# Seven half-size products for four fifths of one block's x^T phi(k), with operand sums on GpSimd and VectorE

## The chip, the cores and the metric

The kernel runs on one core of a Trainium2 chip. The metric is the device time of one execution in microseconds (us); lower is better. A core has five engines that matter here: TensorE (PE in the profile) multiplies matrices into the accumulation memory PSUM, VectorE (DVE), ScalarE (ACT) and GpSimd (POOL) work elementwise, and SyncE (SP) issues DMA transfers. Each engine works through its own queue in order, and semaphores let one wait for another. GpSimd does not read PSUM in this kernel; TensorE reads only SBUF, the memory in which all tiles lie.

## What is computed

Two linear-attention blocks, A and B, read the same input `A_x` and are mixed by a gate. Cut to what matters:

```python
# x: 2048 x 640, wqkv: 640 x 1920, wo: 640 x 640; 32 heads of width 20; all bf16
g = sigmoid((x * gate_w).sum(-1, keepdims=True))
def block(x, wqkv, wo):
    q, k, v = split_heads(x @ wqkv)
    phi = lambda t: where(t > 0, t + 1, exp(t)) + 1e-6
    pq, pk = phi(q), phi(k)
    kv  = einsum("bhsd,bhse->bhde", pk, v)        # per head, 20 x 20
    z   = einsum("bhsd->bhd", pk)
    num = einsum("bhqd,bhde->bhqe", pq, kv)
    den = einsum("bhqd,bhd->bhq", pq, z)[..., None] + 1e-6
    return merge_heads(num / den) @ wo
out = g * block(x, A_wqkv, A_wo) + (1 - g) * block(x, B_wqkv, B_wo)
```

## The kernel before, in words

The kernel never forms v. Since kv is the diagonal part of phi(k)^T x Wv, it computes the 640 x 640 matrix G^T = x^T phi(k) once a block (tile `GT`), multiplies it by Wv, keeps the diagonal heads (`KVT`), and folds `wo` into that (`M`). The output is then the normalised phi(q) times `M`.

The 2048 rows of x are 16 chunks of 128, the 640 columns five blocks of 128 (`DT`). `xn` holds x with its rows on the partitions, `xT` its transpose, `pk` phi(k) by chunks, `pqT[0]` and `pqT[1]` the transposed phi(q) of A and of B. Five stages follow one another for each block:

- `k_chunk` (16 times): ten matmuls (L182) give x Wk for a chunk. `phi` empties them: an exponential on ScalarE (L177), then on VectorE the TENSOR_SCALAR step L178 from SBUF to SBUF, and L179, which reads PSUM and that result. The temporary tile `e` has three buffers.
- `q_unit` (ten for each block): ten matmuls of 512 columns (L218), and the same `phi` on 1024 columns. For A, five units come in the middle of the k chunks, after chunk 7. The other five are in `q_pass`, with the gate's columns (`gate_pass`) and the column sums of phi(k) (`z_rows`, L259) after the first of them and `z_pass` after the third.
- `g_pass` (five for each block): one pass gives one 128-row block of x^T phi(k), 16 chunks by two halves of 320 columns, 32 matmuls (L240), and one ScalarE copy into `GT`.
- `rec_pass`: the denominators (L153), multiplied by a gate factor (L330) and inverted on VectorE (L335). `norm_unit`, five for each block, spreads the inverses by eight small matmuls over two PSUM slots (L377); two multiplies per unit (L393) normalise phi(q) in place. In one of the two ScalarE first copies the PSUM result to bf16 (L391), in the other VectorE reads PSUM itself. In `g_all` the units lie between passes and half passes of g.
- `p_diff` (VectorE), then block B's k chunks, between which `kvt_pass` and `m_unit` finish `KVT` and `M` of A.

PSUM is four slots of two banks. `ps` hands them out in turn, or by number: in `g_all` the passes use slots 0 and 1, `rec_pass` slot 2, the units slots 2 and 3. The last stage, the output product, is already done by Strassen's scheme (`Pair`, `p1` to `p7`), with operand sums on VectorE (`add_rows`, L340).

The order of the instructions is the planner's, by priority in the order of the program, except where `tc.manual_schedule()` fixes the order as written. SP issues the loads: three transfers fill the last 12 chunks of `xn` (L519), and the weights of later stages follow. GpSimd builds the identity, the masks and `E4` in the first 10 us (L129 and others) and has nothing after that.

Of the kernel before, what the change touches and what calls it, by code (L numbers as in the profile page):

```python
# [8 lines left out]
P = 128  # L9
FP32 = mybir.dt.float32  # L10
BF16 = mybir.dt.bfloat16
ACT = mybir.ActivationFunctionType
ALU = mybir.AluOpType

S, D, H = 2048, 640, 32
Dh = D // H
DT = D // P
ST = S // P
# [3 lines left out]
HF = D // 2  # L22
# [4 lines left out]
SH = S // 2  # L27
# [3 lines left out]
def kernel(  # L31
# [11 lines left out]
    nc = tc.nc  # L43
# [4 lines left out]
    persist = ctx.enter_context(tc.tile_pool(name="persist", bufs=1))  # L48
    wpool = ctx.enter_context(tc.tile_pool(name="wpool", bufs=1))
    work = ctx.enter_context(tc.tile_pool(name="work", bufs=2))  # L50
# [5 lines left out]
    def ps_raw(name, slot=None):  # L56

        if slot is None:
            slot = turn[0]
            turn[0] = (slot + 1) % 4  # L60
        return psum.tile([P, 4 * HB], BF16, tag=f"ps{slot}", name=name)

    def ps(name, slot=None):

        return ps_raw(name, slot).bitcast(FP32).rearrange("p (b n) -> p b n", b=2)

    xT = persist.tile([P, DT, S], BF16, name="xT")
    xn = persist.tile([P, ST, D], BF16, name="xn")
    pk = persist.tile([P, ST, D], BF16, name="pk")
    pqT = [persist.tile([P, DT, S], BF16, name=f"pqT{b}") for b in "AB"]  # L70
    GT = persist.tile([P, DT, D], BF16, name="GT")
    KVT = persist.tile([P, NJ, D], BF16, name="KVT")
    M = [persist.tile([P, DT, D], BF16, name=f"M{b}") for b in "AB"]
# [6 lines left out]
    gwr = persist.tile([P, DT, H], BF16, name="gwr")  # L80
    zero = persist.tile([P, HB], BF16, name="zero")
    grow = persist.tile([1, D], BF16, name="grow")
    D3 = persist.tile([P, DT, S // 2], BF16, name="D3")
    TM = [None] * 4
    ge = [persist.tile([P, 2 * RB], FP32, name=f"ge{b}") for b in "AB"]

# [10 lines left out]
    wq = [None, None]  # L97
# [7 lines left out]
    for n in range(1, NB):  # L105
# [3 lines left out]
        for c in range(DT):  # L109
            nc.sync.dma_start_transpose(  # L110
                out=xT[:, c, n * HB:(n + 1) * HB], in_=x2[n * HB:(n + 1) * HB, c * P:(c + 1) * P]
# [8 lines left out]
    for sign, base in ((1, 0), (-1, Dh - 1)):  # L120
        nc.gpsimd.affine_select(
            out=maskE[:], in_=maskE[:], pattern=[[sign * P, DT], [-sign * Dh, H]],
# [3 lines left out]
    for r in range(4):  # L126
        rows = slice(32 * r, 32 * r + 32)
        for sign, base in ((1, 0), (-1, Dh - 1)):
            nc.gpsimd.affine_select(  # L129
                out=E4[rows], in_=E4[rows], pattern=[[sign, D]],  # L130
# [43 lines left out]
    def phi(dst, src, n):  # L174

        e = work.tile([P, 2, n], BF16, tag="e", name="e", bufs=3)
        nc.scalar.activation(out=e[:], in_=src, func=ACT.Exp)  # L177
        nc.vector.tensor_scalar(e[:], e[:], 1.0, EPS, op0=ALU.min, op1=ALU.add)  # L178
        nc.vector.scalar_tensor_tensor(out=dst, in0=src, scalar=1.0 + EPS, in1=e[:], op0=ALU.add, op1=ALU.max)  # L179
# [32 lines left out]
    def q_unit(b, m, h):  # L212

        pt = ps(f"q{'AB'[b]}")
        for u in range(2):
            for c in range(DT):
                n = 2 * h + u
                nc.tensor.matmul(  # L218
                    pt[:, u, :], lhsT=wq[b][:, c, m * P:(m + 1) * P], rhs=xT[:, c, n * HB:(n + 1) * HB],
                    start=(c == 0), stop=(c == DT - 1),  # L220
                )
        phi(pqT[b][:, m, h * 2 * HB:(h + 1) * 2 * HB].rearrange("p (b n) -> p b n", b=2), pt, HB)

    def evac(dst, pt, eng):

        copy = nc.scalar.copy if eng == "act" else nc.vector.tensor_copy
        copy(out=dst.rearrange("p (b n) -> p b n", b=2), in_=pt[:, :, 0:HF])

    def g_pass(b, c, slot, between=None):

        pt = ps(f"g{'AB'[b]}", slot)
        for i in range(ST):
            if between is not None and i == ST // 2:
                between()
            for hf in range(2):
                g_mm(c, i, hf, pt)
        evac(GT[:, c, :], pt, "act")

    def g_mm(c, i, hf, pt):
        nc.tensor.matmul(  # L240
            pt[:, hf, 0:HF], lhsT=xn[:, i, c * P:(c + 1) * P], rhs=pk[:, i, hf * HF:(hf + 1) * HF],
            start=(i == 0), stop=(i == ST - 1),
        )
# [68 lines left out]
    def m_half(b, c, hf, dst):  # L312

        for k, j in enumerate((c, c + 1)):
# [3 lines left out]
                rhs=wo_sb[b][:rows, j, hf * HF:(hf + 1) * HF], start=(k == 0), stop=(k == 1),  # L318
            )

    def rec_pass(b, zsel, slot):

        pt = ps(f"den{'AB'[b]}", slot)
        for h in range(2):
            by_group(pt[:, 0, h * RB:(h + 1) * RB], zsel, pqT[b], h)
        rts = []
        for h in range(2):
            part = slice(h * RB, (h + 1) * RB)
            d1 = work.tile([P, RB], FP32, tag="d1", name="d1")
            nc.vector.scalar_tensor_tensor(  # L330
                out=d1[:], in0=pt[:, 0, part], scalar=EPS, in1=ge[b][:, part], op0=ALU.add, op1=ALU.mult
            )
            rT = work.tile([P, RB], BF16, tag="rT", name="rT")
            with nc.allow_low_precision(reason="a fp32 reciprocal, stored as the bf16 that multiplies bf16"):
                nc.vector.reciprocal(out=rT[:], in_=d1[:])  # L335
            rts.append(rT)
        return rts

    def add_rows(dst, a, b, op):
        nc.vector.tensor_tensor(out=dst, in0=a, in1=b, op=op)  # L340

    def p_diff():

        for rows in (slice(0, HB), slice(HB, SH)):
            up = slice(SH + rows.start, SH + rows.stop)
            add_rows(D3[:, :, rows], pqT[0][:, :, rows], pqT[0][:, :, up], ALU.subtract)

# [24 lines left out]
    def norm_unit(b, parts, rts, slots):  # L372

        pts = [ps(f"ex{'AB'[b]}", s) for s in slots]
        for k, (m, h) in enumerate(parts):
            for j in range(4):
                nc.tensor.matmul(  # L377
                    pts[j // 2][:, j % 2, k * RB:(k + 1) * RB], lhsT=E4[32 * j:32 * j + 32, m * P:(m + 1) * P],
                    rhs=rts[h][32 * j:32 * j + 32, :], start=True, stop=True,
                )  # L380
        (m0, h0), (m1, h1) = parts
        for jj in range(2):
            src = pts[jj][:].rearrange("p j (k n) -> p j k n", n=RB)
            if h0 == h1:
                r0 = h0 * 2 * HB + jj * HB
                dst = pqT[b][:, m0:m1 + 1, r0:r0 + HB].rearrange("p k (j n) -> p j k n", n=RB)
            else:
                dst = pqT[b][:, m0, :].rearrange("p (k u j n) -> p u j k n", k=2, u=2, n=RB)[:, jj]
            if jj == 1:
                ex = work.tile([P, 2, 2, RB], BF16, tag="ex", name="ex")  # L390
                nc.scalar.copy(out=ex[:], in_=src)  # L391
                src = ex[:]
            nc.vector.tensor_tensor(out=dst, in0=src, in1=dst, op=ALU.mult)  # L393
# [6 lines left out]
    def prod(dst, left, right, i, first):  # L400

        r0 = i * P
        for c in range(DT):
            nc.tensor.matmul(  # L404
                dst, lhsT=left[:, c, r0:r0 + P], rhs=right[:, c, :], start=(first and c == 0), stop=(c == DT - 1), skip_group_check=not first,
            )
# [7 lines left out]
    class Pair:  # L414
# [17 lines left out]
        def p7(self):  # L432
            prod(self.at("y"), D3, TM[2], self.i, True)

# [27 lines left out]
    def load_w(b, which, eng):  # L462
        lo = {"q": 0, "k": D, "v": 2 * D}[which]
        t = wpool.tile([P, DT, D], BF16, tag="w" + which, name=f"w{which}{'AB'[b]}")
        eng.dma_start(out=t[:], in_=wq_dram[b][:, :, lo:lo + D])
        return t
# [8 lines left out]
    def q_pass(b, units):  # L475

        units = list(units)
        q_unit(b, *units.pop(0))
        if b == 0:
            gate_pass()  # L480
        zr = z_rows(b)
        for k in range(2):
            q_unit(b, *units.pop(0))
        zsel = z_pass(b, zr)
        for m, h in units:
            q_unit(b, m, h)
        return zsel

    def g_all(b, zsel):

        units = [((m, h), (m + 1, h)) for h in range(2) for m in (0, 2)] + [((DT - 1, 0), (DT - 1, 1))]

        def norm():
            norm_unit(b, units.pop(0), rts, (2, 3))

        g_pass(b, 0, 1)
        rts = rec_pass(b, zsel, 2)
        g_pass(b, 1, 0)
        for c in range(2, DT):
            norm()  # L500
            if b == 1 and c == DT - 1:
                g_last(b, c, (1, 0))
            else:
                g_pass(b, c, (c + 1) % 2, norm if c < DT - 1 else None)
        assert not units
# [12 lines left out]
    for n in range(1, NB):  # L518
        nc.sync.dma_start(  # L519
            out=xn[:, n * CB:(n + 1) * CB, :], in_=x2[n * HB:(n + 1) * HB, :].rearrange("(q p) d -> p q d", p=P)  # L520
        )
    wv[0] = load_w(0, "v", nc.sync)
    load_wo(0, nc.sync)
    wk[1] = load_w(1, "k", nc.sync)
    zsel = q_pass(0, [(m, 1) for m in range(DT)])
    wq[1] = load_w(1, "q", nc.sync)
    g_all(0, zsel)
    p_diff()


# [11 lines left out]
    zsel = q_pass(1, [(m, h) for h in range(2) for m in range(DT)])  # L542
    for tag, ks in (("wk", (0, 3)), ("wq", (1, 2))):
        t = wpool.tile([P, 2, DT, HF], BF16, tag=tag, name="TM" + tag)
# [12 lines left out]
    with tc.manual_schedule():  # L557
# [35 lines left out]
        for i in range(1, half):  # L593
            p, after = pairs[i], pairs[i + 1] if i + 1 < half else None
# [45 lines left out]
```

## Time and profile before

| | |
|---|---|
| Median of 3 runs | 199.96 us (199.86 to 199.97) |
| Profiled execution | 200.22 us, of it 198.4 us span |
| Granted TensorE clock | 1.00 |
| DMA | 14.21 MB, mean 72 GB/s |
| PE busy 0 to 10 us | 8.40 us |
| PE busy 45 to 100 us | 55.00 us |
| VectorE busy 40 to 60 us (A's second half of q, start of g) | 3.10, 3.33, 3.76 and 2.24 us by 5 us |
| VectorE busy 60 to 75 us (A's g passes and normalisation) | 4.17, 3.61 and 3.52 us by 5 us |
| GpSimd busy | 8.60 us, all before 10 us |
| The three loads of `xn` | issued at 25.6 to 26.7 us, landing 4.9 to 7.3 us later |

Times are those of the profiled execution, counted from the start of its span. "Busy" counts instructions at work, not waits. Matmuls are pipelined: one of 320 columns is shown with 299 ns, but they follow each other faster, so their price is read from the length of a whole pass. Weight loads (PEld) overlap the matmuls. Spans on POOL are rough.

### The profile page before, as it was taken

Reading aid. Unit: us, or ns where it says so; the run is one execution under the profiler, and the core shown is the slowest. Engines: PE = TensorE matmul, PEld = TensorE weight load, DVE = VectorE, ACT = ScalarE, POOL = GpSimd, SP = SyncE. Lnnn points to the kernel's source line nnn. Section 1 sums busy time; section 2 is a strip of 40 time slices with the busy share of each in tenths; the row PEclk is TensorE's granted clock in tenths of the full one; section 3 lists DMA queues with packets and bytes.
Section 4 is the critical chain, followed back from the end, with each engine's and each line's share of the span. In section 5 each row is a group of like instructions: output and inputs, shape, how many; then the busy total and the mean of one; then the engine's idle time right before and its main releaser. Section 6 shows DMA issues by size and latency. Waiting matters only on the chain.

```text
span 198.4 us, 3643 instructions
## 1 busy us (share of the span) xinstructions
PE 192.7 (97%) x1521; PEld 123.2 (62%) x1527; DVE 140.2 (71%) x222; ACT 75.7 (38%) x104; POOL 8.6 (4%) x22
## 2 busy tenths in 40 slices
PE   7999999999999999999999999999999999999992
PEld 2666457654576667877774444576667777777771
DVE  3378678866748778667678777748779797886453
ACT  2444455453412443366653445412443421111210
POOL 7900000000000000000000000000000000000000
PEclk9999999999999999999999999999999999999999
DMA  5669479950040000040044000000000002212221
GB/s 191 186 174 170 100 191 372 230 169 3 6 161 3 0 0 3 10 156 3 0 109 82 0 0 0 0 5 0 3 0 0 3 0 81 85 68 76 83 75 67
DMA packets 18015, 14.21 MB, mean 72 GB/s; under 512 B 8735, under 2 KB 17744, under 8 KB 18000
## 3 DMA queue, kind: packets, MB, share of 16 engines
q1 hardware_dynamic: 17566, 13.50, 25.5%
q10 hardware_dynamic: 434, 0.49, 0.8%
q8 instruction: 12, 0.20, 0.4%
q14 instruction: 3, 0.02, 0.0%
HBM read 9.40 MB, written 2.62 MB: 61 GB/s over the span
## 4 chain that ended last, share of the span: by engine, by line
PE 92%; DMA 3%; SPq 3%; issue 0%; DVE 0%
PE gA L240 11%; PE gB L240 11%; PE kB L182 11%; PE qA L218 11%; PE qB L218 11%; PE kA L182 8%; PE oz L404 5%; PE ox L404 5%; PE oy L404 5%; PE ow L404 3%; SPq L110 3%; DMA wkA<-in_A_wqkv_dram 2%; DMA xT<-in_A_x_dram 2%; PE mA L316 1%; PE exB L377 1%; PE exA L377 1%
## 5 line engine op out<-in xcount | busy, mean ns | idle before, releaser
L182 PEld LDWEIGHTS <-xT 128*128 128x128 bf16 x320 | 30.8, 98 | 13.4 <-DVE xT L172 0.8
L240 PEld LDWEIGHTS <-xn 128*128 128x128 bf16 x320 | 30.3, 98 | 14.1 <-issue 2.5
L178 DVE TENSOR_SCALAR e<-e 128x640 bf16<-128x640 bf16 (+1 forms) x52 | 18.9, 364 | 19.3 <-ACT e L177 17.9
L182 PE MATMUL kA<-wkA,xT 128*128 128x320 bf16 x160 | 22.8, 299 | 0.7 <-DMA xT<-in_A_x_dram 0.3
L240 PE MATMUL gA<-pk,xn 128*128 128x320 bf16 x160 | 22.9, 299 | 0.0
L240 PE MATMUL gB<-pk,xn 128*128 128x320 bf16 x160 | 22.9, 299 | 0.0
L182 PE MATMUL kB<-wkB,xT 128*128 128x320 bf16 x160 | 22.9, 299 | 0.0
L218 PE MATMUL qA<-xT,wqA 128*128 128x512 bf16 x97 | 22.1, 379 | 0.2
L218 PE MATMUL qB<-xT,wqB 128*128 128x512 bf16 x97 | 21.9, 379 | 0.2
L218 PEld LDWEIGHTS <-wqB 128*128 128x128 bf16 x100 | 9.6, 98 | 11.4 <-issue 0.3
L218 PEld LDWEIGHTS <-wqA 128*128 128x128 bf16 x100 | 9.6, 97 | 11.3 <-issue 0.3
L177 ACT ACTIVATE e<-kA 128x640 bf16<-128x640 f32 x16 | 11.3, 705 | 11.7 <-PE kA L182 11.7
L177 ACT ACTIVATE e<-kB 128x640 bf16<-128x640 f32 x16 | 11.3, 704 | 11.7 <-PE kB L182 11.7
L177 ACT ACTIVATE e<-qA 128x1024 bf16<-128x1024 f32 x10 | 10.2, 1023 | 13.2 <-PE qA L218 13.2
L177 ACT ACTIVATE e<-qB 128x1024 bf16<-128x1024 f32 x10 | 10.2, 1023 | 13.1 <-PE qB L218 10.7
L179 DVE SCALAR_TENSOR_TENSOR pk<-kB,e 128x640 bf16<-128x640 f32 x16 | 13.2, 825 | 1.6
L179 DVE SCALAR_TENSOR_TENSOR pk<-kA,e 128x640 bf16<-128x640 f32 x16 | 13.2, 824 | 1.5
L179 DVE SCALAR_TENSOR_TENSOR pqTB<-qB,e 128x1024 bf16<-128x1024 f32 x10 | 12.2, 1225 | 1.3 <-DVE e L178 0.5
L179 DVE SCALAR_TENSOR_TENSOR pqTA<-qA,e 128x1024 bf16<-128x1024 f32 x10 | 12.3, 1225 | 1.0
L438 ACT COPY u<-ox 128x320 f32<-128x320 f32 x8 | 3.4, 426 | 20.9 <-PE ox L404 20.9
L404 PEld LDWEIGHTS <-xT 128*128 128x128 bf16 x80 | 7.8, 98 | 3.0
L404 PEld LDWEIGHTS <-pqTB 128*128 128x128 bf16 x80 | 7.8, 98 | 3.0
(94 smaller groups left out, 214.2 us busy)
## 6 DMA issues: line engine op xcount, KB each, us to landing
out_dram<-osb SPq DMA_DIRECT2D x15, 160.0 KB, 1.8
xn<-in_A_x_dram SPq DMA_DIRECT2D x3, 640.0 KB, 6.0
wqA<-in_A_wqkv_dram SPq DMA_DIRECT2D x1, 800.0 KB, 5.1
wvA<-in_A_wqkv_dram SPq DMA_DIRECT2D x1, 800.0 KB, 9.7
wkB<-in_B_wqkv_dram SPq DMA_DIRECT2D x1, 800.0 KB
wqB<-in_B_wqkv_dram SPq DMA_DIRECT2D x1, 800.0 KB, 4.6
wvB<-in_B_wqkv_dram SPq DMA_DIRECT2D x1, 800.0 KB, 4.7
woA<-in_A_wo_dram SPq DMA_DIRECT2D x1, 750.0 KB, 11.9
```

Source lines behind the costliest of these rows:

```text
L110: nc.sync.dma_start_transpose(out=xT[:, c, n * HB:(n + 1) * HB], in_=x2[n * HB:(n + 1) * HB, c * P:(c + 1) * P])
L177: nc.scalar.activation(out=e[:], in_=src, func=ACT.Exp)
L178: nc.vector.tensor_scalar(e[:], e[:], 1.0, EPS, op0=ALU.min, op1=ALU.add)
L179: nc.vector.scalar_tensor_tensor(out=dst, in0=src, scalar=1.0 + EPS, in1=e[:], op0=ALU.add, op1=ALU.max)
L182: nc.tensor.matmul(pt[:, hf, 0:HF], lhsT=xT[:, c, i * P:(i + 1) * P], rhs=wk[b][:, c, hf * HF:(hf + 1) * HF], start=(c == 0), stop=(c == D ...
L218: nc.tensor.matmul(pt[:, u, :], lhsT=wq[b][:, c, m * P:(m + 1) * P], rhs=xT[:, c, n * HB:(n + 1) * HB], start=(c == 0), stop=(c == DT - 1),)
L240: nc.tensor.matmul(pt[:, hf, 0:HF], lhsT=xn[:, i, c * P:(c + 1) * P], rhs=pk[:, i, hf * HF:(hf + 1) * HF], start=(i == 0), stop=(i == ST - 1),
L316: nc.tensor.matmul(dst, lhsT=KVT[:rows, j, c * P:(c + 1) * P], rhs=wo_sb[b][:rows, j, hf * HF:(hf + 1) * HF], start=(k == 0), stop=(k == 1),)
L377: nc.tensor.matmul(pts[j // 2][:, j % 2, k * RB:(k + 1) * RB], lhsT=E4[32 * j:32 * j + 32, m * P:(m + 1) * P], rhs=rts[h][32 * j:32 * j + ...
L404: nc.tensor.matmul(dst, lhsT=left[:, c, r0:r0 + P], rhs=right[:, c, :], start=(first and c == 0), stop=(c == DT - 1), skip_group_check=not ...
L438: nc.scalar.copy(out=self.u2[:], in_=self.at("x"))
```

## The change

For A only, the row blocks 0 to 3 of x^T phi(k), a 512 x 640 matrix, are no longer computed by four passes of g. x's columns 0 to 511 and phi(k) are each cut into two by two blocks: x by column halves of 256 and by chunks 0 to 7 and 8 to 15, phi(k) by the same chunks and by column halves of 320. Strassen's scheme in its seven-product form gives the four quarters of the result; each product is `g_prod`, eight chunks by two row blocks, 16 matmuls. Row block 4 stays a `g_pass`, now the first of them.

- The sums of x (`x_sums`, four of 128 x 2048 bf16) are put on GpSimd, behind the loads of `xn`. They lie in the tiles `D3`, `M[0]` and `M[1]`, which hold nothing yet.
- The sums of phi(k) (`k_sum`, four of 128 x 2560 bf16) are put on VectorE: the first before `q_pass`, the second and third after its last two units, the fourth after the first `norm_unit`. They lie in `pqT[1]`.
- Counted in the order of `g_strassen`, products 1, 3, 5 and 7 run in slot 0, the others in slot 1; products 3, 4, 6 and 7 accumulate on a bank whose earlier content has been read out, and products 1, 2 and 5 start one anew. Two ScalarE copies and five VectorE adds out of PSUM bring the results into `GT` or into three fp32 temporaries (`gt`).
- A `norm_unit` lies after products 2, 3, 4, 5 and 6. For A both its PSUM results now go through a ScalarE copy.
- `q_pass` and `g_all` of A are under `manual_schedule`.

```diff
@@ -80,7 +80,15 @@
     gwr = persist.tile([P, DT, H], BF16, name="gwr")
     zero = persist.tile([P, HB], BF16, name="zero")
     grow = persist.tile([1, D], BF16, name="grow")
-    D3 = persist.tile([P, DT, S // 2], BF16, name="D3")
+    D3 = persist.tile([P, DT, SH], BF16, name="D3")
+    d3_flat = D3[:].rearrange("p c s -> p (c s)")
+    m_flat = [t[:].rearrange("p c d -> p (c d)") for t in M]
+    hc, ic = ST // 2, 2 * P
+    SX = {k: t[:, o:o + hc * ic].rearrange("p (i c) -> p i c", i=hc)
+          for k, t, o in ((1, d3_flat, 0), (2, d3_flat, hc * ic), (3, m_flat[0], 0), (4, m_flat[1], 0))}
+    t_flat = pqT[1][:].rearrange("p c s -> p (c s)")
+    TK = {k: t_flat[:, n * hc * HF:(n + 1) * hc * HF].rearrange("p (i d) -> p i d", i=hc)
+          for n, k in enumerate((1, 2, 3, 4))}
     TM = [None] * 4
     ge = [persist.tile([P, 2 * RB], FP32, name=f"ge{b}") for b in "AB"]
 
@@ -318,6 +326,72 @@
                 rhs=wo_sb[b][:rows, j, hf * HF:(hf + 1) * HF], start=(k == 0), stop=(k == 1),
             )
 
+    def x_sums():
+
+        x11, x21 = [xn[:, 0:hc, k:k + ic] for k in (0, ic)]
+        x12, x22 = [xn[:, hc:ST, k:k + ic] for k in (0, ic)]
+        for dst, a, b, op in (
+            (SX[1], x21, x22, ALU.add), (SX[2], SX[1], x11, ALU.subtract),
+            (SX[3], x11, x21, ALU.subtract), (SX[4], x12, SX[2], ALU.subtract),
+        ):
+            nc.gpsimd.tensor_tensor(out=dst, in0=a, in1=b, op=op)
+
+    def k_sum(k):
+
+        b11, b12 = [pk[:, 0:hc, n * HF:(n + 1) * HF] for n in range(2)]
+        b21, b22 = [pk[:, hc:ST, n * HF:(n + 1) * HF] for n in range(2)]
+        a, b = {1: (b12, b11), 2: (b22, TK[1]), 3: (b22, b12), 4: (b21, TK[2])}[k]
+        add_rows(TK[k], a, b, ALU.subtract)
+
+    def g_prod(pt, left, right, first):
+
+        for i in range(hc):
+            for n in range(2):
+                nc.tensor.matmul(
+                    pt[:, n, 0:HF], lhsT=left[:, i, n * P:(n + 1) * P], rhs=right[:, i, :],
+                    start=(first and i == 0), stop=(i == hc - 1), skip_group_check=not first,
+                )
+
+    def g_strassen(norm):
+
+        x11, x12 = [xn[:, k:k + hc, 0:ic] for k in (0, hc)]
+        x22 = xn[:, hc:ST, ic:2 * ic]
+        b11 = pk[:, 0:hc, 0:HF]
+        b21, b22 = [pk[:, hc:ST, n * HF:(n + 1) * HF] for n in range(2)]
+        lo, hi = slice(0, HF), slice(HF, D)
+
+        def temp(name):
+            return work.tile([P, 2, HF], FP32, tag="gt", name=name, bufs=3)
+
+        def add(dst, pt, sb):
+            nc.vector.tensor_tensor(out=dst, in0=pt[:, :, 0:HF], in1=sb[:], op=ALU.add)
+
+        even, odd = ps("gs0", 0), ps("gs1", 1)
+        g_prod(even, x11, b11, True)
+        p1 = temp("p1")
+        nc.scalar.copy(out=p1[:], in_=even[:, :, 0:HF])
+        g_prod(odd, SX[2], TK[2], True)
+        u2 = temp("u2")
+        add(u2[:], odd, p1)
+        norm()
+        k_sum(4)
+        g_prod(even, x12, b21, False)
+        nc.scalar.copy(out=GT[:, 0:2, lo], in_=even[:, :, 0:HF])
+        norm()
+        g_prod(odd, SX[3], TK[3], False)
+        u3 = temp("u3")
+        add(u3[:], odd, p1)
+        norm()
+        even = ps("gs0", 0)
+        g_prod(even, SX[1], TK[1], True)
+        add(GT[:, 2:4, hi], even, u3)
+        norm()
+        g_prod(odd, x22, TK[4], False)
+        add(GT[:, 2:4, lo], odd, p1)
+        norm()
+        g_prod(even, SX[4], b22, False)
+        add(GT[:, 0:2, hi], even, u2)
+
     def rec_pass(b, zsel, slot):
 
         pt = ps(f"den{'AB'[b]}", slot)
@@ -386,7 +460,7 @@
                 dst = pqT[b][:, m0:m1 + 1, r0:r0 + HB].rearrange("p k (j n) -> p j k n", n=RB)
             else:
                 dst = pqT[b][:, m0, :].rearrange("p (k u j n) -> p u j k n", k=2, u=2, n=RB)[:, jj]
-            if jj == 1:
+            if jj == 1 or b == 0:
                 ex = work.tile([P, 2, 2, RB], BF16, tag="ex", name="ex")
                 nc.scalar.copy(out=ex[:], in_=src)
                 src = ex[:]
@@ -482,8 +556,10 @@
         for k in range(2):
             q_unit(b, *units.pop(0))
         zsel = z_pass(b, zr)
-        for m, h in units:
+        for k, (m, h) in enumerate(units):
             q_unit(b, m, h)
+            if b == 0:
+                k_sum(2 + k)
         return zsel
 
     def g_all(b, zsel):
@@ -493,6 +569,12 @@
         def norm():
             norm_unit(b, units.pop(0), rts, (2, 3))
 
+        if b == 0:
+            g_pass(b, DT - 1, 1)
+            rts = rec_pass(b, zsel, 2)
+            g_strassen(norm)
+            assert not units
+            return
         g_pass(b, 0, 1)
         rts = rec_pass(b, zsel, 2)
         g_pass(b, 1, 0)
@@ -519,12 +601,15 @@
         nc.sync.dma_start(
             out=xn[:, n * CB:(n + 1) * CB, :], in_=x2[n * HB:(n + 1) * HB, :].rearrange("(q p) d -> p q d", p=P)
         )
+    x_sums()
     wv[0] = load_w(0, "v", nc.sync)
     load_wo(0, nc.sync)
     wk[1] = load_w(1, "k", nc.sync)
-    zsel = q_pass(0, [(m, 1) for m in range(DT)])
-    wq[1] = load_w(1, "q", nc.sync)
-    g_all(0, zsel)
+    k_sum(1)
+    with tc.manual_schedule():
+        zsel = q_pass(0, [(m, 1) for m in range(DT)])
+        wq[1] = load_w(1, "q", nc.sync)
+        g_all(0, zsel)
     p_diff()
```

## The prediction, made before the changed kernel ran

> **What bounds the kernel now.** I read the page first, for engines and chain.
>
> ```profile
> PE 192.7 (97%) x1521; PEld 123.2 (62%) x1527; DVE 140.2 (71%) x222; ACT 75.7 (38%) x104; POOL 8.6 (4%) x22
> ...
> PE 92%; DMA 3%; SPq 3%; issue 0%; DVE 0%
> ```
>
> PE (TensorE) is busy for the whole span and is 92% of the chain that ended last: what leaves PE's queue is time gained, and any new wait of PE is time lost. DVE (VectorE) has 29% idle, POOL (GpSimd) nearly all.
>
> Next, the groups by form, for prices (columns: count, busy us, mean ns, idle before):
>
> ```profile
> L240 PE MATMUL gA<-pk,xn 128*128 128x320 bf16 x160 | 22.9, 299 | 0.0
> ...
> L178 DVE TENSOR_SCALAR e<-e 128x640 bf16<-128x640 bf16 x32 | 10.4, 325 | 8.0 <-ACT e L177 6.5
> L178 DVE TENSOR_SCALAR e<-e 128x1024 bf16<-128x1024 bf16 x20 | 8.5, 427 | 11.4 <-ACT e L177 11.4
> ...
> L393 DVE TENSOR_TENSOR pqTA<-exA,pqTA 128x1024 bf16<-128x1024 f32 x5 | 6.1, 1225 | 3.5 <-PE exA L377 3.5
> ...
> L393 DVE TENSOR_TENSOR pqTA<-ex,pqTA 128x1024 bf16<-128x1024 bf16 x5 | 3.4, 688 | 0.3
> ...
> L340 DVE TENSOR_TENSOR D<-pqTA 128x2560 bf16<-128x2560 bf16 x2 | 2.9, 1484 | 0.0
> ```
>
> The L178 step of phi gains 384 elements for 102 ns, 0.27 ns each. The two-input bf16 form goes at 0.52 ns, and the forms that read PSUM (L179: 825 ns at 640, 1225 at 1024) at 1.04 ns. So L178 moves SBUF data about four times as fast as the PSUM forms; remember that below.
>
> Then the timeline of the part the change works in.
>
> ```profile
> 40.76 0.33 DVE L178 TENSOR_SCALAR e<-e 128x640 bf16<-128x640 bf16 x1 [0.46 <-ACT e L177]
> 41.19 0.82 DVE L179 SCALAR_TENSOR_TENSOR pk<-kA,e 128x640 bf16<-128x640 f32 x1
> ...
> 43.18 1.26 PE L259 MATMUL zA<-pk,ones 128*32 128x320 bf16 x32
> ...
> 57.58 1.28 PE L153 MATMUL denA<-pqTA,zsel 128*32 128x256 bf16 x40
> ...
> 58.91 0.76 DVE L330 SCALAR_TENSOR_TENSOR d<-denA,geA 128x256 f32<-128x256 f32 x2 [2.76 <-PE denA L153]
> ...
> 74.01 4.52 PE L240 MATMUL gA<-pk,xn 128*128 128x320 bf16 x32
> ...
> 78.37 2.88 PE L182 MATMUL kB<-wkB,xT 128*128 128x320 bf16 x20
> ```
>
> Chunk 15's phi ends at 42.01, 1.2 us before the column sums that read it; VectorE idles 2.76 us before the denominators; one pass of 32 matmuls takes 74.01 to 78.37.
>
> **Part 1, the matmuls.** Four passes of 32 (128) become seven products of 16 (112), of the same form; the fifth block stays a pass. A pass is 4.36 us, so a matmul is 0.136 us, and 16 fewer give 2.18 us, all on the path. Weight loads fall alike and stay under the matmuls.
>
> **Part 2, what empties PSUM.** ScalarE loses four 0.69 us copies and gets two (P1, C11). VectorE gets five adds of 640 fp32 elements out of PSUM: nearest row L179, 0.82 us, so 4.1 us. In five normalisation units the 1.22 us PSUM multiply becomes a 1.02 us ScalarE copy and a 0.69 us multiply: VectorE minus 2.7, ScalarE plus 5.1 us. A product and a unit last 2.18 + 0.43 = 2.61 us of PE; in that time ScalarE needs 2.04, with P1 or C11 2.73, so the second PSUM slot of the next unit may come free 0.1 us late. I count 0.2 (0 to 0.5). A product that accumulates on a bank just read (P3, P4, P6, P7 on what P1, P2, P5 left) waits for that read, but a whole product or a unit always lies between (at least 2.2 us against 0.7 to 1.7), so nothing. The price without that cover would be 0.8 us a time.
>
> **Part 3, the sums of phi(k).** Four of 128x2560 at 1.484 us (L340), 5.9 us of VectorE. The first stands ahead of the q units, where VectorE has a quarter idle. The second and third come behind the last two units' phi. The fourth unit's phi ends at 54.0, so the second sum runs to 55.5, the last phi to 57.2 instead of 56.15, still 0.3 us ahead of the denominators at 57.58; the third then ends at 58.7, ahead of L330. The 2.76 us idle hides them; without it, up to 1.5 us. The fourth is queued behind the first unit's multiplies, some 6 us ahead of its product. At the end the last add (P7 ends near 76.2) pushes the two p_diff subtractions to about 77.1 to 80.1, so B's first phi starts some 1.5 us after it could; four PSUM slots take most of it up: 0.3 (0 to 0.6).
>
> Scratch reuse waits for nothing: D3, M and the second pqT are written again at 77, 84 and 105 us by the trace. SP's queue has the same loads in the same order.
>
> So without part 4: minus 2.18, plus 0.2, plus 0.3, is minus 1.7 us (minus 2.2 to minus 1.1).
>
> **Part 4, the sums of x on GpSimd.** Four TENSOR_TENSOR of 128x2048 bf16, two inputs each, one behind another. They need the last xn load, issued at 26.7 and landing 7.3 us later at the longest: start near 34. GpSimd's queue holds nothing behind them. No row shows a two-input GpSimd operation, so I bound it. One input and one output: L129's 640 elements at 0.71 us against 0.34 for L121's 160 is 0.77 ns an element on about 0.22. If both reads overlapped, 2048 elements would take 1.8 us; with two passes 3.35; if read, read and write queue, 4.9. Reads that share one way are the nearest to what a one-input row shows, and the write may or may not hide, so I take 4.1, and 1.8 to 4.9 for the range. Done by about 51 us in any case, and the first user (the second product) is at 61: GpSimd's own time is hidden.
>
> What is not hidden is VectorE beside it. The trace shows the two side by side in one place only:
>
> ```profile
> 8.44 0.71 POOL L129 TENSOR_SCALAR_AFFINE_SELECT E<-E 32x640 bf16<-32x640 bf16 x1
> ...
> 9.09 0.33 DVE L178 TENSOR_SCALAR e<-e 128x640 bf16<-128x640 bf16 x1
> ...
> 9.21 0.78 POOL L129 TENSOR_SCALAR_AFFINE_SELECT E<-E 32x640 bf16<-32x640 bf16 x1
> ```
>
> L178 comes at the very end of one GpSimd operation and is not delayed; the GpSimd operation that starts during it takes 0.78 instead of 0.71. So something gave, on the side that came second. The opposite order, L178 arriving early in a long GpSimd operation, is not in the trace. The bounds of one such meeting are 0 and the rest of that operation. I take the wait as the likelier: L178 is the fastest SBUF form there is here, and its 0.27 ns against 1.04 leaves little room for a second reader.
>
> [...]
>
> Price of the wait: four operations at 4.1 with three L178 steps of 0.33 slipped between them fill 34.0 to 51.4. One phi gets through per 4.4 us instead of per 1.36. In the trace L178 starts for chunks 11 to 15 at 35.05, 36.36, 37.72, 39.12 and 40.76; now 11, 12, 13 go at 38.1, 42.5, 47.0, 14 at 51.4, and 15 one phi (1.2) later at 52.6: 11.8 us late. PE can run on until its four PSUM slots are full, but the column sums (43.18) stand in PE's queue ahead of four of the five q units and read chunk 15. Taking off their 1.2 us of slack, PE is 10.6 late there. Afterwards PE (2.2 us a q unit) paces VectorE (1.65), so it is not won back. With part 1 to 3's minus 1.7: plus 8.9, so I say 200.22 + 8.9 = 209.1 for the profiled execution (span 198.4). The median, 199.96, is 0.26 lower: **208.8**.
>
> **The rivals.** *Waits as above* (the forecast). Each 0.1 us of a GpSimd operation is worth 0.4 us; ends: 1.8 us gives plus 8.9 - 9.2, about 0; 4.9 gives plus 12.1, 211.8 on the median's scale. For it: fourfold rate of L178, the stretched 0.78. Against: L178 itself never shows a delay.
>
> *No waits, or short ones*: VectorE and GpSimd share without blocking, or L178 merely halves its speed (some twelve steps by 0.3 us, 3.6 us, within VectorE's idle quarter and four slots). Then minus 1.7: 199.96 - 1.7 = 198.3, range 197.7 to 198.9. For it: 0.326 us for L178 at 9.09, exactly as elsewhere. It decides wherever a meeting costs VectorE less than some 0.6 us (1.7 us gained and 1.2 us of slack, over the five steps of chunks 11 to 15).
>
> *Waits, but short operations* (1.8 to 2.5 us): loss and gain nearly cancel, 199.7 to 202.5; break-even is at about 1.9 us an operation. For it: overlapped reads, which no row excludes.
>
> *The products wait for the sums of x* even without blocking: that needs over 13 us per operation (34 to 61 for the second), against all bounds; under 2%, within the high end.
>
> **How the numbers follow.** Waits with long operations 0.62, short operations 0.08, no waits 0.30. The likeliest case alone spans 203 to 212.5. The range of 197.7 to 212.5 reaches from the faster case to that end, leaving out some 0.05 below and 0.10 above. A difference of 0.2% (0.4 us) is about what a measurement here can tell from none. Faster: 0.30 and a sliver of the short operations, 0.31; same 0.03; slower 0.66.
>
> **What would show it.** Right: between 34 and 52 us L178 starts some 4 us apart, each at a GpSimd operation's end, while PE idles before chunk 14, chunk 15 or the column sums, released by VectorE; four GpSimd operations of 3.4 to 5 us; from the denominators to B's first matmul some 18.6 us instead of 20.8. Wrong: L178 stays at its 1.2 to 1.4 us pace beside GpSimd; then the end is near 198.3. If that later stretch is not 2 us shorter, parts 1 to 3 are wrong, most likely by a PSUM slot that VectorE or ScalarE frees late.

## The result, and the profile after

The changed kernel takes 209.97 us (209.41 to 210.34) against 199.97 us (the median of four runs): a ratio of 1.0489 (95% interval 1.0476 to 1.0502), 10.0 us slower. The profiled execution is the 209.41 us one, 9.2 us over the 200.22 us one of before; its span is 207.5 us against 198.4. It is the fastest of the four, and what follows accounts for it alone: no trace shows where the median's other 0.6 us are. The forecast was 208.8 us.

The page first, the same lines as before (engines; then the chain that ended last, by engine and by line):

```profile
PE 193.9 (93%) x1505; PEld 123.2 (59%) x1511; DVE 158.0 (76%) x231; ACT 79.1 (38%) x107; POOL 24.8 (12%) x26
...
PE 87%; DVE 10%; issue 1%; ACT 0%; DVEq 0%
PE gB L248 11%; PE kB L190 10%; PE qA L226 10%; PE qB L226 10%; PE gs L350 8%; DVE e L186 7%; PE kA L190 6%; PE oz L478 5%; PE ox L478 5%; PE oy L478 5%; PE ow L478 3%; DVE pk L187 2%; PE gA L248 2%; PE warm L145 2%; PE mA L324 1%; PE exA L451 1%
```

Sixteen of TensorE's matmuls are gone, and a piece of VectorE has come into the chain: `DVE e L186`, the TENSOR_SCALAR step of phi (L178 before). VectorE's busy time rose by 17.8 us, more than the sums and adds that it got. The groups by form say where (count, busy us, mean ns):

```profile
L186 DVE TENSOR_SCALAR e<-e 128x640 bf16<-128x640 bf16 x32 | 22.2, 696 | 4.2 <-ACT e L185 3.2
L187 DVE SCALAR_TENSOR_TENSOR pk<-kA,e 128x640 bf16<-128x640 f32 x16 | 13.2, 825 | 1.9 <-DVE e L186 0.5
```

The first took 325 ns on the mean and 10.4 us in all; now 11.8 us more. The second, which reads PSUM, is what it was. The timeline shows which of the 32 they are:

```profile
30.76 4.06 POOL L337 TENSOR_TENSOR MA<-xn 128x2048 bf16<-128x2048 bf16 x1 [20.87 <-issue]
...
31.67 3.34 DVE L186 TENSOR_SCALAR e<-e 128x640 bf16<-128x640 bf16 x1
...
34.78 4.14 POOL L337 TENSOR_TENSOR D<-xn 128x2048 bf16<-128x2048 bf16 x1
35.11 0.82 DVE L187 SCALAR_TENSOR_TENSOR pk<-kA,e 128x640 bf16<-128x640 f32 x1
35.85 3.25 DVE L186 TENSOR_SCALAR e<-e 128x640 bf16<-128x640 bf16 x1
...
40.08 2.15 PE L190 MATMUL kA<-wkA,xT 128*128 128x320 bf16 x10 [2.57 <-DVE pk L187]
...
49.50 1.52 PE L190 MATMUL kA<-wkA,xT 128*128 128x320 bf16 x10 [0.89 <-DVE pk L187]
...
52.25 0.32 DVE L186 TENSOR_SCALAR e<-e 128x640 bf16<-128x640 bf16 x1
...
54.41 1.26 PE L267 MATMUL zA<-pk,ones 128*32 128x320 bf16 x32
...
68.81 1.27 PE L161 MATMUL denA<-pqTA,zsel 128*32 128x256 bf16 x40
...
87.49 2.88 PE L190 MATMUL kB<-wkB,xT 128*128 128x320 bf16 x20
```

Read it in pairs. L186 starts 0.9 to 1.1 us into a GpSimd sum and is recorded until 0.2 us after that sum's end; L187 then runs beside the next sum in its usual 0.82 us; the next L186 is caught again. Four steps take 3.34, 3.25, 3.28 and 3.28 us: four waits of 3.0 us, which the profile books as busy time of VectorE, not as idle. TensorE runs ahead until its PSUM slots are full and then stands (2.57 us before one chunk). Chunk 15's L186 comes at 52.25 instead of 40.76, the denominators at 68.81 instead of 57.58, 11.23 us late. From there to B's first matmul it is 18.68 us instead of 20.79: the half-size products do gain, 2.11 us. 11.23 less 2.11 is 9.12 of the 9.2 us: hardly anything is left over.

### The profile page after: what moved, and what is told of

Its sections match the earlier page's. It is cut to its first block, busy times and chain, and to the rows that moved or that the text cites. A ratio compares the mean times of both kernels' runs of the same rounds, so it can differ in the third digit from the quotient of the medians.

```text
span 207.5 us, 3640 instructions
## 1 busy us (share of the span) xinstructions
PE 193.9 (93%) x1505; PEld 123.2 (59%) x1511; DVE 158.0 (76%) x231; ACT 79.1 (38%) x107; POOL 24.8 (12%) x26
## 4 chain that ended last, share of the span: by engine, by line
PE 87%; DVE 10%; issue 1%; ACT 0%; DVEq 0%
PE gB L248 11%; PE kB L190 10%; PE qA L226 10%; PE qB L226 10%; PE gs L350 8%; DVE e L186 7%; PE kA L190 6%; PE oz L478 5%; PE ox L478 5%; PE oy L478 5%; PE ow L478 3%; DVE pk L187 2%; PE gA L248 2%; PE warm L145 2%; PE mA L324 1%; PE exA L451 1%
## 5 line engine op out<-in xcount | busy, mean ns | idle before, releaser
L190 PEld LDWEIGHTS <-xT 128*128 128x128 bf16 x320 | 31.8, 100 | 21.5 <-issue 7.8
L186 DVE TENSOR_SCALAR e<-e 128x640 bf16<-128x640 bf16 (+1 forms) x52 | 30.7, 592 | 13.4 <-ACT e L185 12.4
L190 PE MATMUL kA<-wkA,xT 128*128 128x320 bf16 x160 | 25.3, 317 | 7.2 <-DVE pk L187 7.1
L248 PEld LDWEIGHTS <-xn 128*128 128x128 bf16 x192 | 18.3, 98 | 8.4 <-issue 1.3
L226 PEld LDWEIGHTS <-wqA 128*128 128x128 bf16 x100 | 9.6, 98 | 11.5 <-issue 0.5
L187 DVE SCALAR_TENSOR_TENSOR pk<-kA,e 128x640 bf16<-128x640 f32 x16 | 13.2, 825 | 1.9 <-DVE e L186 0.5
L187 DVE SCALAR_TENSOR_TENSOR pk<-kB,e 128x640 bf16<-128x640 f32 x16 | 13.1, 824 | 1.4
L187 DVE SCALAR_TENSOR_TENSOR pqTA<-qA,e 128x1024 bf16<-128x1024 f32 x10 | 12.2, 1224 | 1.0
L187 DVE SCALAR_TENSOR_TENSOR pqTB<-qB,e 128x1024 bf16<-128x1024 f32 x10 | 12.3, 1225 | 1.0
L465 ACT CAST ex<-exA 128x1024 bf16<-128x1024 f32 x10 | 9.6, 1017 | 3.7 <-PE exA L451 3.7
L478 PEld LDWEIGHTS <-xT 128*128 128x128 bf16 x80 | 7.8, 98 | 3.0
```

What stands on the lines that cost most here:

```text
L190: nc.tensor.matmul(pt[:, hf, 0:HF], lhsT=xT[:, c, i * P:(i + 1) * P], rhs=wk[b][:, c, hf * HF:(hf + 1) * HF], start=(c == 0), stop=(c == D ...
L226: nc.tensor.matmul(pt[:, u, :], lhsT=wq[b][:, c, m * P:(m + 1) * P], rhs=xT[:, c, n * HB:(n + 1) * HB], start=(c == 0), stop=(c == DT - 1),)
L248: nc.tensor.matmul(pt[:, hf, 0:HF], lhsT=xn[:, i, c * P:(c + 1) * P], rhs=pk[:, i, hf * HF:(hf + 1) * HF], start=(i == 0), stop=(i == ST - 1),
L478: nc.tensor.matmul(dst, lhsT=left[:, c, r0:r0 + P], rhs=right[:, c, :], start=(first and c == 0), stop=(c == DT - 1), skip_group_check=not ...
```

## The experiments

The theory: while GpSimd is at work on SBUF, VectorE's fast step from SBUF waits until that GpSimd instruction has ended. The first rival puts the loss on the phi(k) sums and the order by hand; the second on traffic, bytes that the engines share, whatever the length of an instruction.

**The GpSimd sums alone** (e1, into the kernel before):

```diff
+    x_sums()                      # four GpSimd sums, as in the change; nobody reads them
     wv[0] = load_w(0, "v", nc.sync)
```

> The kernel before, with nothing of the change but the four GpSimd sums of x, whose results nobody reads. Waiting theory (each fast VectorE step waits for the end of the GpSimd operation in progress): in the changed kernel PE reached the denominators 11.2 us late, so about 11.2 us over the kernel before, 211.2 us, with four TENSOR_SCALAR steps of 3.3 us. Rival (the loss comes from the phi(k) sums on VectorE and the written order, GpSimd beside it does no harm): 200.0 us.

Measured: 212.08 us, ratio 1.0617 (1.0583 to 1.0651). L183, the same step there, takes 2.94, 3.24, 3.28 and 3.28 us. The loss is there without one product, phi(k) sum or written order. It is 0.9 us larger than expected; the denominators come at 69.56, 11.98 us late, 0.75 later than in the changed kernel, with a granted TensorE clock that stayed low for longer (see the end).

**The change without the sums of x** (e2):

```diff
-    x_sums()
-    SX = {1: ..., 2: ..., 3: ..., 4: ...}      # in D3, M
+    SX = {k: xn[:, o:o + hc, c:c + ic] for k, o, c in ((1, 0, ic), (2, 0, 0), (3, hc, 0), (4, hc, ic))}
```

> The changed kernel without the sums of x: the products read blocks of xn itself in their place, so the output is another; all else is kept. Waiting theory: the gain of the half-size products appears, some 2.1 us from the denominators to B's first matmul, 197.9 us. Rival (phi(k) sums and written order cost the time): about 209 us, as with the sums.

Measured: 197.97 us, ratio 0.9898 (0.9881 to 0.9915). All else in the change costs less than it gains. The first rival falls with these two.

**The sums of x on VectorE, same place** (e3):

```diff
-            nc.gpsimd.tensor_tensor(out=dst, in0=a, in1=b, op=op)
+            nc.vector.tensor_tensor(out=dst, in0=a, in1=b, op=op)
```

> The changed kernel with the four sums of x on VectorE, written at the same place, so that the planner puts them in its queue. Waiting theory: no GpSimd, no waits; VectorE gets four steps of about 1.2 us (2048 elements at 0.52 ns on 0.16), 4.9 us in all, in the stretch where it is 85% busy, so part of it delays PE through the PSUM slots: 198 to 201 us, 199.5 if about a third shows. Rival (any engine's reading of xn there slows the others, or the order does): 205 us or more.

Measured: 216.74 us, ratio 1.0836 (1.0817 to 1.0855): a miss for the theory, and inside what the rival had said. But not for the rival's reason. Among who waited for whom (us in all, times, the longest):

```profile
DVE MA L337 <- DMA xn<-in_A_x_dram: 16.7, 1, 16.7
...
PE kA L190 <- DVE pk L187: 16.0, 1, 16.0
```

The planner put the first sum into VectorE's queue in front of phi, 16.7 us ahead of the load that it reads, and everything behind it stood. The run says nothing on the theory; it is tried again below.

**The same GpSimd work in 16 pieces** (e4):

```diff
-            nc.gpsimd.tensor_tensor(out=dst, in0=a, in1=b, op=op)
+            for i in range(0, hc, 2):
+                nc.gpsimd.tensor_tensor(out=dst[:, i:i + 2], in0=a[:, i:i + 2], in1=b[:, i:i + 2], op=op)
```

> The changed kernel with each GpSimd sum cut into four instructions of 512 elements, 16 in all, the same bytes. Waiting theory, by instruction: a piece takes about 0.22 + 512 x 1.88 ns = 1.2 us, a fast VectorE step waits 0.3 to 0.6 us instead of 3.0, one phi goes through per 1.4 to 1.6 us beside PE's 1.36, so 198.5 to 201 us. Rival (the two engines share a bandwidth, so that bytes count and not the length of an instruction): about 209 us as before.

Measured: 198.35 us, ratio 0.9912 (0.9897 to 0.9928). The timeline of this kernel, on GpSimd and VectorE:

```profile
34.27 0.35 DVE L186 TENSOR_SCALAR e<-e 128x640 bf16<-128x640 bf16 x1
34.40 2.42 POOL L338 TENSOR_TENSOR D<-D,xn 128x512 bf16<-128x512 bf16 x2
34.73 0.82 DVE L187 SCALAR_TENSOR_TENSOR pk<-kA,e 128x640 bf16<-128x640 f32 x1
35.47 0.35 DVE L186 TENSOR_SCALAR e<-e 128x640 bf16<-128x640 bf16 x1
```

The two engines fall into step: each piece takes 1.15 to 1.23 us, as long as one phi, and for five phis in a row L186 slips in between two pieces, with hardly a wait (0.35 us). At the beginning and the end of the pieces single steps do wait, 0.5 to 0.8 us each (this is the slowest of the five executions, 199.25 us). Same bytes, same arithmetic, 11.6 us less: what counts is the length of an instruction, and the second rival falls.

**GpSimd memsets instead of sums** (e5, kernel before; 4.15 us each, writing only):

```diff
+        for k in range(4):
+            nc.gpsimd.tensor_tensor(out=SX[3][:, k, 0:2], in0=xn[:, 4 + k, 0:2], in1=xn[:, 8 + k, 0:2], op=ALU.add)
+            nc.gpsimd.memset(d3_flat[:, 0:4864], 0.0)
```

> The kernel before plus, in place of the four sums, four GpSimd memsets of 4864 bf16 elements (0.2 + 4864 x 0.82 ns = 4.2 us each) behind tiny two-column adds that wait for xn; nobody reads them. They write SBUF as long as the sums did and read none. [...] Variant (only GpSimd's reads stand in the way of the fast VectorE step): 200.0 us.

Measured: 209.91 us, ratio 1.0506 (1.0489 to 1.0524). The planner moved two of the memsets ahead of the adds, so they do not lie as I had meant: one at 3.6 us, ahead of phi, one at 13.9, and two from 32.2 on. Each of the last three caught a step, of 4.14, 4.03 and 3.02 us, 10.1 us of waiting in all. The first of the three:

```profile
13.92 4.15 POOL L330 MEMSET D<- 128x4864 bf16 x1
...
14.11 4.14 DVE L183 TENSOR_SCALAR e<-e 128x640 bf16<-128x640 bf16 x1
```

So a GpSimd operation that reads nothing held this step up as well, by 2.7 to 3.8 us a time, and the variant's 200.0 us did not come.

**GpSimd copies, one input** (e6, kernel before, 2048 elements each):

```diff
+            nc.gpsimd.tensor_copy(out=SX[k + 1], in_=xn[:, 0:hc, k * P:k * P + ic] ...)
```

> The kernel before plus four GpSimd copies of 2048 bf16 elements, one input, 1.8 us each by 0.77 ns an element, read by nobody. Waiting theory: a fast VectorE step waits some 0.7 us, one phi per 2.1 us for four phis beside PE's 1.36, 3.0 us less the 1.2 us of slack: plus 1.8, 201.8 us. Rival (only operations with two inputs do harm): 200.0 us.

Measured: 202.12 us, ratio 1.0115 (1.0079 to 1.0151). The copies take 1.9 to 2.0 us and three of the four steps beside them 1.08 us, a wait of 0.75.

**The sums of x on VectorE, placed by hand** (e7; the first of several places):

```diff
+        if b == 0:
+            x_sum(1)
         q_unit(b, *units.pop(0))
```

> The sums of x on VectorE again, each written by hand into a gap that the trace shows: the first behind chunk 15's phi, the second behind the zsel copy, the third behind the last q unit, the fourth behind the second normalisation unit; the second sum of phi(k) moves up behind the column sums' multiply. Nothing on GpSimd. If e3 lost its 16.7 us only because its first sum stood in VectorE's queue ahead of phi and waited for xn: VectorE's 4.9 us fit its idle time, 198.0 us (197.7 to 198.6). If VectorE is short of time there: 200 us or more.

Measured: 216.47 us, ratio 1.0828 (1.081 to 1.0846). A miss of the same kind: inside the part in written order the first sum had nothing in front of it, and the planner put the head of that part into VectorE's queue at 16.1 us; it waited 17.2 us for xn.

**No fast step beside GpSimd** (e8; the four long sums stay):

```diff
+        if twice[0]:                            # chunks 8 to 15 and the first q unit after them
+            nc.scalar.activation(out=r[:], in_=src, func=ACT.Relu, scale=-1.0)
+            nc.scalar.activation(out=e[:], in_=r[:], func=ACT.Exp, scale=-1.0)
+        else: ...                               # as before; the gate's two VectorE steps come after zsel
```

> The changed kernel with its four long GpSimd sums, but without the VectorE step that waits: for chunks 8 to 15 and the first q unit after them phi's minimum is taken by ScalarE (Relu of -x, then Exp of the negated result; the added 1e-6 is left out there), so VectorE keeps only the step that reads PSUM, and the gate's two VectorE steps come after zsel. Waiting theory: the GpSimd sums still take 4.1 us each and hurt nobody; ScalarE needs 1.41 us a chunk beside PE's 1.36, so 198.0 to 199.0 us. Rival (GpSimd slows all VectorE or PE work by its traffic): 205 us or more.

Measured: 198.01 us, ratio 0.9907 (0.9892 to 0.9922). The timeline:

```profile
34.27 4.07 POOL L343 TENSOR_TENSOR D<-xn 128x2048 bf16<-128x2048 bf16 x1
34.36 0.69 ACT L188 ACTIVATE r<-kA 128x640 bf16<-128x640 f32 x1
34.49 0.82 DVE L193 SCALAR_TENSOR_TENSOR pk<-kA,e 128x640 bf16<-128x640 f32 x1 [0.54 <-ACT e L189]
35.08 0.74 ACT L189 ACTIVATE e<-r 128x640 bf16<-128x640 bf16 x1
...
57.65 1.27 PE L161 MATMUL denA<-pqTA,zsel 128*32 128x256 bf16 x40
...
76.33 2.88 PE L196 MATMUL kB<-wkB,xT 128*128 128x320 bf16 x20
```

GpSimd's sums take 4.07 us three times and 4.29 once, VectorE's PSUM form beside them keeps its 0.82 us, ScalarE's two steps take 0.69 and 0.74 us, and TensorE is at the denominators 0.07 us after the kernel before. With the step that waits gone, the whole loss is gone, although GpSimd's sums are still there. VectorE is also spared the steps themselves, but e2, which keeps them and has no GpSimd sums, is as fast.

**The sums on VectorE behind the first q unit's phi** (e9; the first of several places):

```diff
         zr = z_rows(b)
+        if b == 0:
+            x_sum(1)
```

> As e7, but no sum of x can be put ahead of an earlier phi: the first is written behind the column sums' multiply (so behind the first q unit's phi), the second behind the fourth q unit's, the third after the denominators, the fourth as in e7. e7 lost its time at its first sum, which the planner put into VectorE's queue at 16.1 us, 17.2 us ahead of its load. If that was all: 198.0 us (197.7 to 198.6), as e8, with nothing on GpSimd. If VectorE is short of time: 199 us or more.

Measured: 198.40 us, ratio 0.9924 (0.991 to 0.9937); denominators at 57.40, B's first matmul at 76.08. VectorE has room for all eight sums; e3 and e7 lost their time to the place in its queue.

**Which VectorE forms wait?** The four sums (e10), and then three memsets (e11), held back by a small add that reads an inverse, so that they lie beside A's normalisation in the kernel before:

```diff
         rts = rec_pass(b, zsel, 2)
+        if b == 0:
+            x_sums(rts[1])
```

> The kernel before plus the four GpSimd sums, read by nobody, held back until the inverses are done (63 us), so that they lie beside A's normalisation: there VectorE has no one-input fast step, but multiplies and two p_diff subtractions with both inputs in SBUF. If only the one-input fast step waits: 200.0 us. If forms with two SBUF inputs wait too: one unit per 4.3 us instead of 2.6 while the sums last (63 to 80), some 6 us late, less 2 to 3 us of slack: 203 to 205 us, with L393 multiplies of up to 4 us.

Measured: 204.35 us, ratio 1.0216 (1.0203 to 1.023). With the sums:

```profile
67.12 4.39 POOL L335 TENSOR_TENSOR D<-D,xn 128x2048 bf16<-128x2048 bf16 x1
67.52 1.21 DVE L409 TENSOR_TENSOR pqTA<-exA,pqTA 128x1024 bf16<-128x1024 f32 x1
...
68.65 3.41 DVE L409 TENSOR_TENSOR pqTA<-ex,pqTA 128x1024 bf16<-128x1024 bf16 x1
...
73.25 0.40 PE L393 MATMUL exA<-rT,E 32*128 32x256 bf16 x8 [1.79 <-DVE pqTA L409]
```

The multiply with one input in PSUM keeps its time (1.21 to 1.23 us); the one with both inputs in SBUF takes 3.41 instead of 0.69 us (three times; a fourth time 2.99), and the next sum, which starts before that multiply ends (67.12 against 67.60 us), 4.39 instead of 4.06.

> As e10 with three GpSimd memsets (4.2, 2.8 and 2.8 us) in place of the sums: GpSimd writes SBUF and reads none. If a VectorE form with two SBUF inputs stands in the way of GpSimd's reads alone: 200.0 us and multiplies of 0.69 us. If it waits for any GpSimd operation: two or three multiplies of 2.5 to 4 us, 200.5 to 202.5 us.

Measured: 200.01 us, ratio 0.9998 (0.9987 to 1.0009). With the memsets:

```profile
63.51 4.15 POOL L330 MEMSET D<- 128x4864 bf16 x1
63.67 1.23 DVE L404 TENSOR_TENSOR pqTA<-exA,pqTA 128x1024 bf16<-128x1024 f32 x1 [0.74 <-PE exA L388]
64.98 0.69 DVE L404 TENSOR_TENSOR pqTA<-ex,pqTA 128x1024 bf16<-128x1024 bf16 x1
```

The same multiply, in the midst of a memset: 0.69 us. So the form with two SBUF inputs waited for the sums, which read and write (2.3 to 2.7 us), and not for memsets, which only write, while the fast one-input step (e5) waited for memsets too (2.7 to 3.8 us).

## Why the prediction was right, step by step

**The bound.** TensorE's path set the end, as said; a wait of VectorE came into it, and the chain shows it.

**Part 1** (2.18 us gained): 2.11 us between the denominators and B's first matmul, 18.68 us against the 18.6 named in advance.

**Parts 2 and 3** (0.2 and 0.3 lost): both oversized. Three of the four intervals from one normalisation unit to the next are 2.61 us as before, one is 2.67 or 2.68: 0.07 us instead of 0.2. From B's first matmul to the end of the span it is 120.0 us in both profiles, so the later p_diff cost nothing, where I had left 0.3: VectorE's first step of B's phi comes 3.9 us after B's first matmul instead of 2.3, as foreseen, and TensorE goes on without a wait. The two phi(k) sums behind the last q units did fit in VectorE's idle time: with no waits (e8) the denominators come 0.07 us late. The sum without part 4 was minus 1.7 us; e2 shows minus 2.0, e8 minus 1.9. My no-wait rival, 198.3 us with a range of 197.7 to 198.9, is what those two, e4 and e9 measured; it failed as a forecast of the change only because the waits are real.

**Part 4, length.** 4.1 us, taken between bounds of 1.8 and 4.9: measured 4.05 to 4.14. Its parts: pieces of 512 elements take 1.15 us, so 1.89 ns an element on about 0.18. One-input copies of as many elements take half, 1.9 to 2.0 us (e6).

**Part 4, start.** I had it wait for the last load of xn, near 34 us. The planner put the third sum first, x11 - x21, which needs only the first of the loads, and it began at 30.76. So chunks 8 to 11 were caught, not 11 to 14, and TensorE stood before chunks 12 to 15. That changed the place, not the price: four operations, four waits.

**Part 4, price.** Four waits of 3.0 us are 11.8; chunk 15's fast step comes at 52.25 (said: 52.6), 11.5 us late; TensorE is 11.2 us late at the gate's columns, the column sums and the denominators (said: 10.6); nothing is won back after, as said. What I had wrong is where the lateness passes to TensorE. I had it wait at the column sums for chunk 15's phi, and took off the 1.2 us of slack there. It never waited there: its last wait, 0.89 us, was for the PSUM slot of chunk 15's matmuls, which began at 49.50 instead of 38.45, 11.05 us late. Behind them it had its own work up to the column sums at 54.41, and chunk 15's phi was through at 53.49, with 0.9 us of the slack unused. With 2.1 gained: plus 9.2 in the profiled execution, said 8.9. The terms that are off, 0.6 in the lateness and 0.4 in parts 2 and 3, work against each other; that the sum came within 0.3 us is in part luck.

Some figures of the prediction are off by their own terms: plus 8.9 on 199.96 is 208.9, the end for 4.9 us an operation is 212.1 and not 211.8, and four operations of 4.9 us would have run until 54.6, not 51. None changes the argument.

**The choice between waiting and not** rested on one row, a GpSimd operation 0.07 us longer, and on a rate. That was thin: 0.30 was left for no waits. It is settled now by e1 and e8 from both ends. What waited, form by form: the fast one-input step waited for sums (3.0 us), copies (0.75) and memsets (up to 3.8); the form with two SBUF inputs waited for sums (2.3 to 2.7) and not for memsets (0.69 us beside them); a form with one SBUF input, reading PSUM, showed no wait (0.82 us in the mean of 16 in the changed kernel, 1.21 in e10).

## What to carry to other kernels

Work on GpSimd is not free because GpSimd is idle (four sums that nobody reads: ratio 1.0617 in e1): price it by the VectorE steps beside it that are of a form that waited here (TENSOR_SCALAR from SBUF, and beside sums a multiply with two SBUF inputs). Each GpSimd sum that caught the TENSOR_SCALAR step cost VectorE what was left of the sum, 3.0 of 4.1 us. If such work has to lie there, cut it into pieces no longer than VectorE's own cycle (pieces of 1.15 to 1.23 us beside a phi of 1.2: 198.35 us instead of 209.97 for the same work), or leave VectorE only the form that reads PSUM meanwhile (0.82 us beside the sums as without them: 198.01, without the added 1e-6 there), or place the work on VectorE behind something that is surely later than its load (198.40). All three beat the kernel before by 0.8 to 0.9%, and the sums of x themselves then cost some 0.4 us at most beside the 197.97 us without them.

And look at a queue's head: a step that waited for a load held everything behind it on its engine, for 16.7 us in e3 and 17.2 in e7, though the step itself takes 1.23.

## What the runs showed of the hardware that was not expected

A VectorE instruction that is held up by GpSimd is recorded as running: 3.3 us for a step of 0.33, with the idle time of the engine falling (before this group 4.2 us instead of 8.0). Busy shares do not show such waits; a group's mean against its known duration does (696 against 325 ns).

TensorE's granted clock fell while it stood, from 1.00 to 0.60 and 0.54. By stretches of four us (TensorE busy, weight loads, VectorE, ScalarE, GpSimd; then the clock), in the changed kernel:

```profile
36.00:40.00 4.00, 1.50 (x10) 0.96 (x10) 3.90 (x3) 0.71 (x1) 3.92 (x2) 1.00 0.98 184
40.00:44.00 4.00, 2.15 (x10) 1.19 (x10) 3.90 (x3) 0.70 (x1) 3.92 (x2) 0.60 0.03 9
44.00:48.00 4.00, 2.83 (x10) 1.42 (x10) 3.90 (x3) 0.70 (x1) 3.17 (x1) 0.54 0.00 0
48.00:52.00 4.00, 2.68 (x19) 1.70 (x20) 3.36 (x8) 1.41 (x2) 0.00 (x0) 1.00 0.01 2
```

Ten matmuls of a chunk took 2.83 us at 0.54 instead of 1.52 at full clock. There it cost nothing, since the next step waited for VectorE anyway. With the sums alone (e1) the clock was still 0.72 from 48 to 52 us and 0.85 from 52 to 56, where TensorE was the one waited for. The traces show what this cost: at chunk 15's matmuls e1 is still 0.73 us ahead of the changed kernel (48.77 against 49.50); from there to the gate's columns the same matmuls take 5.29 us, in the stretches with the 0.72 and the 0.85, against 3.81 at 1.00; and from the gate's columns to the denominators both take 15.50. So the 0.75 us that e1 is later arise in this stretch.
